# The remainder of the pooled keys in halves of the array's rows, two products of 64 rows in place of each two of 128

## The chip, the core and the metric

The kernel runs on one core of a Trainium2 chip. A core has a matrix engine (TensorE, PE in the profile; its weight loads are listed apart as PEld), three engines for elementwise work (VectorE or DVE, ScalarE or ACT, GpSimd or POOL) and a queue engine (SyncE, SP) that here issues all the transfers. The time of a kernel is the time on the device in microseconds (us); a lower one is better. All times here are of this one core.

## The reference

Attention over pooled keys, followed by a two-layer network with a rational function between the layers. All in float32.

```python
# q, k, v: [8 batches, 8 heads, 576, 64]
k_p = k.reshape(B, H, 72, 8, D).mean(axis=3)      # 72 pooled keys
v_p = v.reshape(B, H, 72, 8, D).mean(axis=3)
scores = scale * np.matmul(q, k_p.transpose(0, 1, 3, 2))
scores = scores - np.max(scores, axis=-1, keepdims=True)
attn = np.exp(scores)
attn = attn / (np.sum(attn, axis=-1, keepdims=True) + 1e-09)
x = np.matmul(attn, v_p)        # -> [4608 tokens, 512]
h = x @ w_in                    # 512 x 2048
P = a[0] + a[1] * h + a[2] * h**2 + a[3] * h**3
Q = 1.0 + np.abs(b[0]) * np.abs(h) + np.abs(b[1]) * h**2
out = (P / (Q + 1e-6)) @ w_out  # 2048 x 512
```

## The kernel before

**Blocks.** The 4608 tokens are 18 blocks of 256 (`TOK`). A batch has 576 tokens, so 12 blocks lie within one batch and 6 straddle two (`segs` then gives two pieces of 64, 128 or 192 tokens). For each block `attend(i)` makes the attention output `x`, transposed, as a high and a low part (`xs`, two tiles in fp32r, the format in which TensorE takes a product in one pass); then eight steps u follow, each with `mm1` (24 products into a bank `ph`), `rational` (ACT, POOL and DVE) and `mm2` (24 products with the weights `wout` into the two banks `po`).

**Attention of a block.** Heads go in four pairs j. A tile of 128 queries gets its scores in banks `ps` (products with the pooled keys `kpT`, full float32, two passes each), then maximum, exponential, sum and quotient on DVE, ACT and POOL in the tile `e`. A pair of heads has 2 x 72 = 144 pooled keys. 128 of them fill the rows of the array; 16 (`REM`) are left over. The probabilities are turned so that the keys lie on the rows: by products with the identity (`pm`, `pr`) in the first four blocks, by DVE transposes and small transfers (`am<-e`) in the later ones. `am0` holds the high parts, `am1` the low parts and, behind them, two columns of tiles for the remainder.

**The remainder before.** For each two pairs (c = 0, 1) the 16 + 16 left-over keys stand four times on the 128 rows: row 32 g + 16 m + r is copy g of key r of pair 2c + m. The copies carry high and low parts, of the probabilities in `am1` and of the values in `vr`, so that one product gives the sum of the part products. `vr` has one 128 x 64 tile for each pair j, in which the rows of the other pair are zero (masks `mrem_lo[m]`, `mrem[m]`, made by `make_masks`, lines 398 to 418; `split_v`, lines 592 to 598, uses them on ACT and DVE).

**`values(i, hi, lo)`** (lines 707 to 729) is where the block's output is summed. There are two banks `pv`, one for each c. For each bank, each jj and each piece of tokens four products follow each other: high values x high probabilities, low x high, the remainder, high x low.

```python
terms = ((o, vh[:, j, :], hi[:, j, r0:r1]), (o, vl[:, j, :], hi[:, j, r0:r1]),
         (pv[:D, jj, r0:r1], vr[n % 2][:, j, :], lo[:, NJ + c, r0:r1]),
         (o, vh[:, j, :], lo[:, j, r0:r1]))
```

The remainder has 128 rows and 64 columns (the left-over keys belong to the first head of the pair), all others 128 x 128. A block has 16 products, or 32 if it straddles, of which 4 or 8 are remainders: 12 x 4 + 6 x 8 = 96 in all. The bank of one c goes to `x` by an ACT copy and a DVE subtraction while the other c is on TensorE. In the built program the instructions name the row groups and column groups of the array that they use. The remainder names all four of both, as the 128 x 128 products do; a straddling tile's `ps` products name two of the four column groups (64 queries each), and `pl`, the last 64 rows of the pooled keys in `prep_k`, names two of the four row groups.

**What sets the order.** `Plan` collects every operation with an estimated cost and a due time, and `solve` sets them in order on each engine by a simulation with these costs. Before that `shift` moves the due times of a random 3% of the first 1850 operations, once for each seed in `SHIFTS` (line 111). Where the plan sees TensorE idle up to the first products of `values`, and here and there later, `issue` puts in filler products (line 276: `idle<-identr`, `po<-zero`). All recorded operations have line 284.

Of the kernel before, what the change touches and what calls it, by code (L numbers as in the profile page):

```python
# [100 lines left out]
class Plan:  # L101
# [9 lines left out]
    SHIFTS = (600170, 650652, 293686, 721265, 222299, 972752, 932340, 238443, 467684, 409349, 642869, 707107)  # L111
# [191 lines left out]
def tile_pooled_attention_then_rational_moe(  # L303
# [80 lines left out]
    masks = new("cpool", "masks", [P, 6], F32, "masks")  # L384
# [6 lines left out]
    mrem_lo, mrem = ([masks[:, i + m:i + m + 1] for m in range(2)] for i in (2, 4))  # L391
# [6 lines left out]
    def make_masks():  # L398
        def band(m, lo, hi):

            small("memset", m, 1.0 / G)
            if lo > 0:
                small("affine_select", out=m, in_=m, pattern=[[0, 1]], compare_op=ALU.is_ge,
                      fill=0.0, base=-lo, channel_multiplier=1)
            if hi < P:
                small("affine_select", out=m, in_=m, pattern=[[0, 1]], compare_op=ALU.is_ge,
                      fill=0.0, base=hi - 1, channel_multiplier=-1)

        band(mlo, 0, SP - REM)
        band(mhi, SP - REM, P)  # L410

        for m in range(2):
            for g in range(4):
                band(bands[:, g:g + 1], g * 32 + m * REM, g * 32 + (m + 1) * REM)
            small("tensor_tensor", out=mrem_lo[m], in0=bands[:, 1:2], in1=bands[:, 3:4],
                  op=ALU.add)
            small("tensor_tensor", out=mrem[m], in0=bands[:, 0:1], in1=bands[:, 2:3], op=ALU.add)
            small("tensor_tensor", out=mrem[m], in0=mrem[m], in1=mrem_lo[m], op=ALU.add)
# [65 lines left out]
    vr = [new("cpool", f"vr{i}", [P, NJ, D], F32R, f"vr{i}") for i in range(2)]  # L484
# [53 lines left out]
    def prep_v_early(n):  # L538
# [11 lines left out]
        for m in range(2):  # L550
            dma(64, place[m * REM:(m + 1) * REM, CW:2 * CW].rearrange("p (c x) -> p c x", c=2),
                rows[m::2, 0:REM, :].rearrange("c r x -> r c x"))
# [5 lines left out]
    def prep_v(n):  # L558
# [4 lines left out]
        for c in (2, 0, 1):  # L563
            place = new("stage", "st", [P, 1024], F32, f"st_v{n}_{c}")
            st = place.rearrange("p (j x) -> p j x", j=2)
            if c < 2:
                dma(512, st, rows[2 * c:2 * c + 2, REM:, :].rearrange("j r x -> r j x"))
            else:
                for g in range(4):
                    for m in range(2):  # L570
                        p0 = g * 32 + m * REM
                        dma(64, place[p0:p0 + REM].rearrange("p (j x) -> p j x", j=2),
                            rows[m::2, 0:REM, :].rearrange("c r x -> r c x"))
# [10 lines left out]
    def split_v(n, vs, vrs, port):  # L584
# [44 lines left out]
    def attention(t, hi, lo, qs, es):  # L629

# [50 lines left out]
        rem = [pairs[:, 2 * c:2 * c + 2, 0:REM].unsqueeze(1).to_broadcast([P, 4, 2, REM])  # L681
               for c in range(2)]
        four = [pairs[:, NJ + c, REM:].rearrange("p (g m r) -> p g m r", g=4, m=2)
# [6 lines left out]
        else:  # L690
# [6 lines left out]
            for c in range(2):  # L697
# [4 lines left out]
            act(2 * P).copy(lo[:, NJ:, col], pr)  # L702
            dve(2 * P).tensor_tensor(
                out=lo[P // 2:, NJ:, col], in0=pr[P // 2:],
                in1=lo[P // 2:, NJ:, col].bitcast(F32), op=ALU.subtract)

    def values(i, hi, lo):

        xs = [new("work2", f"x{s}", [P, NJ, TOK], F32R, f"x{s}_{i}") for s in range(2)]
        for c in range(2):  # L710
            pv = bank(f"pv{i}_{c}", [P, 2, TOK])
            calls = []
            for jj in range(2):
                j = 2 * c + jj
                for r0, r1, n in segs(i * TOK, TOK):
                    vh, vl = vm[n % 2]
                    o = pv[:, jj, r0:r1]
                    terms = ((o, vh[:, j, :], hi[:, j, r0:r1]), (o, vl[:, j, :], hi[:, j, r0:r1]),
                             (pv[:D, jj, r0:r1], vr[n % 2][:, j, :], lo[:, NJ + c, r0:r1]),
                             (o, vh[:, j, :], lo[:, j, r0:r1]))  # L720
                    calls += [mm(dst, vals, probs, s == 0, s == 3)
                              for s, (dst, vals, probs) in enumerate(terms)]
            pe(118 * len(calls), calls, claims=xs)
# [9 lines left out]
    def attend(i):  # L733
# [12 lines left out]
        if i >= 4:  # L746
# [153 lines left out]
    for g in range(4):  # L900
        small("tensor_copy", out=fourfold[:, g * 32:(g + 1) * 32], in_=ident[:2 * REM, :2 * REM])
# [65 lines left out]
```

## Time and profile before

| | us |
|---|---|
| median of 3 runs (lowest, highest) | 943.76 (943.32, 945.35) |
| the profiled execution | 945.64 |
| its span on the core | 943.9 |
| DVE busy in it | 786.0 |
| ACT busy in it | 693.7 |
| POOL busy in it | 528.0 |

The profile is one execution. The median of a group's durations is that of one instruction; products on TensorE are pipelined, so that a product of 256 columns that lasts 0.28 us ends some 0.12 us after the one ahead of it. Costs on TensorE are therefore read from the distance between ends (start plus length of successive rows of the timeline, or the length of a piece in the chain that ended last, divided by its count), not from mean durations. The columns of the views: start, length, engine, line, operation, out<-in, shape (rows * columns of the weights, then the streamed operand), count, and in brackets an idle time and what ended it.

### The profile page before, as it was taken

To read this page: it belongs to the slowest core of one execution; us is meant where nothing else is said; L and a number is where in the kernel's file an instruction comes from. 1 tells how busy PE (TensorE), PEld (TensorE's weight loads), DVE (VectorE), ACT (ScalarE), POOL (GpSimd) and SP (SyncE) were. 2 spreads that over 40 slices of the span, in tenths; PEclk is the share of its full clock that TensorE was granted. 3 is DMA by queue.
4 is the path that set the end of the run, shared out by engine and by line. 5 is a ranking of instruction groups with operands and counts; after the bars stand their busy time and mean duration, and the time that the engine had idled before them with its cause. 6 is when DMAs were issued, how large, how long until landed. Compare 5 with 4: busy or idle time off the path is not lost.

```text
span 943.9 us, 17079 instructions
## 1 busy us (share of the span) xinstructions
PE 932.3 (99%) x6152; PEld 845.0 (90%) x6152; DVE 786.0 (83%) x1336; ACT 693.7 (73%) x1124; POOL 528.0 (56%) x463
## 2 busy tenths in 40 slices
PE   8899999999999999999999999999999999999998
PEld 8888998989988899998999899998999899999996
DVE  7799988788989888887887997888898987887664
ACT  4788889868675877686776777676868595868674
POOL 4776866866446544445634574447545663544443
PEclk9999999999999999999999999999999999999999
DMA  9994201254235322122603160316222421202000
GB/s 275 313 390 160 45 29 46 67 127 87 49 81 105 86 34 47 29 56 53 138 5 75 51 140 8 54 37 139 47 36 50 97 50 28 51 1 57 1 23 23
DMA packets 185365, 75.33 MB, mean 80 GB/s; under 512 B 162624, under 2 KB 162624, under 8 KB 185280
## 3 DMA queue, kind: packets, MB, share of 16 engines
q1 hardware_dynamic: 185280, 74.23, 31.2%
q8 instruction: 49, 0.80, 0.4%
q14 instruction: 36, 0.29, 0.1%
HBM read 50.60 MB, written 12.58 MB: 67 GB/s over the span
## 4 chain that ended last, share of the span: by engine, by line
PE 87%; DMA 3%; SPq 3%; DVE 3%; POOL 1%; ACT 1%; issue 1%; POOLq 0%; ACTq 0%
PE ph L284 39%; PE po L284 39%; PE pv L284 4%; PE ps L284 4%; SPq L284 3%; DMA q<-in_q_dram 1%; DMA early<-in_v_dram 1%; DVE sm L284 1%; DMA st_v<-in_v_dram 1%; DVE t L284 1%; POOL w L284 0%; PE pvs L284 0%; ACT rp L284 0%; PE pq L284 0%; DVE mx L284 0%
## 5 line engine op out<-in xcount | busy, mean ns | idle before, releaser
L284 PEld LDWEIGHTS ph<-x,win 128*128 128x128 f32 x3264 | 472.7, 188 | 55.5 <-ACT w L284 0.8
L284 PE MATMUL ph<-x,win 128*128 128x256 f32 x3264 | 495.7, 282 | 1.4 <-DVE x L284 0.5
L284 PE MATMUL po<-wout,gh 128*128 128x512 f32 x1152 | 353.1, 397 | 0.1
L284 POOL TENSOR_TENSOR w<-w,r 128x512 f32<-128x512 f32 (+1 forms) x145 | 191.1, 1318 | 230.3 <-ACT r L284 228.1
L284 POOL TENSOR_TENSOR gl<-t,gh 128x512 fp32r<-128x512 f32 (+1 forms) x145 | 193.3, 1333 | 93.1 <-ACT gh L284 91.9
L284 PEld LDWEIGHTS po<-wout,gh 128*128 128x128 f32 x1152 | 185.7, 189 | 12.5 <-POOL wout L284 0.8
L284 PE MATMUL po<-wout,gl 128*128 128x512 f32 x576 | 181.8, 396 | 0.3 <-POOL gl L284 0.3
L284 ACT ACTIVATE rp<-w,cbias 128x512 f32<-128x512 f32 (+1 forms) x145 | 99.6, 687 | 59.8 <-POOL w L284 56.6
L284 DVE SCALAR_TENSOR_TENSOR t<-t,abn,rp 128x512 f32<-128x512 f32 (+1 forms) x145 | 107.3, 740 | 38.4 <-ACT rp L284 35.3
L284 DVE TENSOR_TENSOR t<-t,ph 128x512 f32<-128x512 f32 (+1 forms) x145 | 97.8, 675 | 48.7 <-ACT t L284 46.7
L284 ACT ACTIVATE r<-w,abn 128x512 f32<-128x512 f32 (+1 forms) x145 | 117.9, 813 | 20.8 <-POOL gl L284 11.4
L284 ACT ACTIVATE t<-ph,abn 128x512 f32<-128x512 f32 (+1 forms) x145 | 111.0, 767 | 26.3 <-PE ph L284 23.0
L284 ACT ACTIVATE w<-ph 128x512 f32<-128x512 f32 (+1 forms) x145 | 85.7, 591 | 40.8 <-PE ph L284 34.4
L284 DVE SCALAR_TENSOR_TENSOR t<-t,abn,ph 128x512 f32<-128x512 f32 (+1 forms) x145 | 107.0, 738 | 5.2 <-ACT w L284 1.3
L284 ACT CAST gh<-t 128x512 fp32r<-128x512 f32 (+1 forms) x145 | 88.3, 609 | 20.5 <-DVE t L284 16.9
L284 DVE SCALAR_TENSOR_TENSOR t<-rp,t 128x512 f32<-128x512 f32 (+1 forms) x145 | 99.4, 685 | 4.1
L284 DVE SCALAR_TENSOR_TENSOR rp<-w,rp 128x512 f32<-128x512 f32 (+1 forms) x145 | 99.0, 683 | 0.2
L284 PEld LDWEIGHTS po<-wout,gl 128*128 128x128 f32 x576 | 93.0, 189 | 6.4 <-POOL gl L284 0.5
L284 ACT ACTIVATE rp<-rp 128x512 f32<-128x512 f32 (+1 forms) x145 | 84.1, 580 | 3.6 <-DVE t L284 0.5
L284 POOL TENSOR_TENSOR e<-e,sm 128x576 f32<-128x576 f32 x36 | 41.8, 1175 | 51.2 <-DVE sm L284 38.7
L284 POOL TENSOR_TENSOR st_v<-st_v 128x512 f32<-128x512 f32 (+1 forms) x36 | 36.3, 1015 | 17.4 <-DMA st_v<-in_v_dram 10.7
L284 PE MATMUL ps<-kpT,qT 128*128 128x144 f32 (+1 forms) x320 | 45.6, 292 | 0.4 <-DVE kpT L284 0.2
(101 smaller groups left out, 855.9 us busy)
## 6 DMA issues: line engine op xcount, KB each, us to landing
am<-e SPq DMA_DIRECT2D x224, 48.0 KB, 2.1
out_dram<-ob SPq DMA_DIRECT2D x17, 512.0 KB, 3.1
rwin<-in_moe_w_in_dram SPq DMA_DIRECT2D x8, 1024.0 KB, 11.1
rwout<-in_moe_w_out_dram SPq DMA_DIRECT2D x8, 1024.0 KB, 14.1
st_k<-in_k_dram SPq DMA_DIRECT2D x12, 512.0 KB, 4.8
st_v<-in_v_dram SPq DMA_DIRECT2D x12, 512.0 KB, 4.2
q<-in_q_dram SPq DMA_DIRECT2D x144, 32.0 KB, 2.0
st_v<-in_v_dram SPq DMA_DIRECT2D x48, 64.0 KB, 2.2
```

The lines of the kernel that those rows point to most:

```text
L284: getattr(engines[op.eng], name)(*map(value, args), **{k: value(v) for k, v in kw.items()})
```

## The change

The left-over keys are sorted the other way: for jj = 0, 1 the column of tiles holds pairs jj and 2 + jj, and row 64 m + 16 g + r is copy g of key r of pair 2m + jj. So each pair has a half of the rows to itself, `vr` shrinks from four tiles to two, nothing need be zeroed, and a remainder product takes 64 rows. `values` now fills both banks at once, c alternating, so that the two remainder products of one jj, on rows 0 to 63 and 64 to 127 and into different banks, stand next to each other. The number of products stays 384, 96 of them remainders.

```diff
-    SHIFTS = (600170, 650652, 293686, ...)
+    SHIFTS = (945215, 768360, 653776, 414080)
...
-    vr = [new("cpool", f"vr{i}", [P, NJ, D], F32R, f"vr{i}") for i in range(2)]
+    vr = [new("cpool", f"vr{i}", [P, 2, D], F32R, f"vr{i}") for i in range(2)]
...
-        r = vr[n % 2].rearrange("p (c m) x -> p c m x", m=2)
-        for m in range(2):
-            dst = r[:, :, m, :]
-            act(2 * D + 100).activation(dst, vrs, AF.Copy, scale=mrem_lo[m])
-            dve(2 * D, port=port).scalar_tensor_tensor(
-                out=dst, in0=vrs, scalar=mrem[m], in1=dst.bitcast(F32),
-                op0=ALU.mult, op1=ALU.subtract)
+        r = vr[n % 2]
+        act(2 * D + 100).activation(r, vrs, AF.Copy, scale=mrem_lo)
+        dve(2 * D, port=port).scalar_tensor_tensor(
+            out=r, in0=vrs, scalar=1.0 / G, in1=r.bitcast(F32), op0=ALU.mult, op1=ALU.subtract)
...
-        rem = [pairs[:, 2 * c:2 * c + 2, 0:REM].unsqueeze(1).to_broadcast([P, 4, 2, REM])
+        rem = [pairs[:, c:NJ:2, 0:REM].unsqueeze(2).to_broadcast([P, 2, 4, REM])
                for c in range(2)]
-        four = [pairs[:, NJ + c, REM:].rearrange("p (g m r) -> p g m r", g=4, m=2)
+        four = [pairs[:, NJ + c, REM:].rearrange("p (m g r) -> p m g r", g=4, m=2)
                 for c in range(2)]
...
-        for c in range(2):
-            pv = bank(f"pv{i}_{c}", [P, 2, TOK])
+        pvs = [bank(f"pv{i}_{c}", [P, 2, TOK]) for c in range(2)]
+        for jj in range(2):
             calls = []
-            for jj in range(2):
-                j = 2 * c + jj
...
+            sg = segs(i * TOK, TOK)
+            for r0, r1, n in sg:
+                vh, vl = vm[n % 2]
+                for s, (vals, probs) in enumerate(((vh, hi), (vl, hi), (vr[n % 2], lo), (vh, lo))):
+                    for c in range(2):
+                        j = 2 * c + jj
+                        if s == 2:
+                            half = slice(c * (P // 2), (c + 1) * (P // 2))
+                            calls.append(mm(pvs[c][:D, jj, r0:r1], vals[half, jj, :],
+                                            probs[half, NJ + jj, r0:r1], False, False))
+                        else:
+                            calls.append(mm(pvs[c][:, jj, r0:r1], vals[:, j, :],
+                                            probs[:, j, r0:r1], s == 0, s == 3))
+            pe(118 * 7 * len(sg) + 10, calls, claims=xs)
+        for c, pv in enumerate(pvs):
...
-            half = slice(P // 2, P)
-            act(2 * TOK).copy(lo[0:P // 2, NJ:], whole[0:P // 2, NJ:])
-            own = es[half, 0:2, :, 0:P]
-            both = [x[half, NJ:].rearrange("p c (m s) -> p c m s", m=2) for x in (lo, whole)]
-            act(2 * TOK).copy(own.bitcast(F32R), both[1])
+            own = es[:, 0:2, :, 0:P]
+            both = [x[:, NJ:].rearrange("p c (m s) -> p c m s", m=2) for x in (lo, whole)]
+            act(2 * TOK).activation(own.bitcast(F32R), both[1], AF.Copy, scale=one_lo)
             dve(2 * TOK, port=True).tensor_tensor(
                 out=both[0], in0=both[1], in1=own, op=ALU.subtract)
```

High and low copies now lie in both halves of the rows; so the last steps treat all 128 rows and choose by a mask (`one_lo`), where before the upper and the lower 64 rows were treated apart. That takes one ACT operation out of each of the last 14 blocks, and with the smaller `vr` ACT has 22 instructions fewer in all, DVE 8, POOL 10. The transfers are as many and as large as before.

What the change does to the order, at two places. First TensorE in a block within one batch (block 7), the first half of its `values`; `pv_0` and `pv_1` are the banks of the two c, `am` the probabilities, `vm` and `vr` the values. In a row of the order 64x256 is the size of what is written (64 columns of weights, 256 tokens). Before:

```order
L284 MATMUL po_0_1_4436<-wout_1145,gl_3_4591 128x512
L284 MATMUL pv_0_4682<-am_7_4521,vm_863 128x256
L284 MATMUL pv_0_4682<-am_7_4521,vm_906 128x256
L284 MATMUL pv_0_4682<-am_7_4335,vr_808 64x256
L284 MATMUL pv_0_4682<-am_7_4335,vm_863 128x256
L284 MATMUL pv_0_4682<-am_7_4521,vm_863 128x256
L284 MATMUL pv_0_4682<-am_7_4521,vm_906 128x256
L284 MATMUL pv_0_4682<-am_7_4335,vr_808 64x256
L284 MATMUL pv_0_4682<-am_7_4335,vm_863 128x256
L284 MATMUL pv_1_4694<-am_7_4521,vm_863 128x256
```

With the change, at the same place:

```order
L284 MATMUL ph_7_4599<-x_6_4087,win_1864 128x256 x4
L284 MATMUL pv_0_4633<-am_7_4471,vm_843 128x256
L284 MATMUL pv_1_4635<-am_7_4471,vm_843 128x256
L284 MATMUL pv_0_4633<-am_7_4471,vm_922 128x256
L284 MATMUL pv_1_4635<-am_7_4471,vm_922 128x256
L284 MATMUL pv_0_4633<-am_7_4286,vr_977 64x256
L284 MATMUL pv_1_4635<-am_7_4286,vr_977 64x256
L284 MATMUL pv_0_4633<-am_7_4286,vm_843 128x256
L284 MATMUL pv_1_4635<-am_7_4286,vm_843 128x256
```

The two remainder products of a jj stood four apart, each alone between 128-row products; now they are neighbours, and ahead of and behind the two stands a 128 x 128 product. In the built program the first of them names row groups 0 and 1 and the second row groups 2 and 3; both name all column groups. No pair has another pair as its neighbour, so there are 48 such places.

Second, TensorE at the start, where the first block's `values` meets `pq` (the turning of the second block's queries, which waits for the transfer of `q`; `pr` is the last turning of the first block's probabilities, `idle` are fillers). Before:

```order
L284 MATMUL pr_344<-identr,e_240 128x128 x2
L276 MATMUL idle<-identr 128x256 x22
L284 MATMUL idle<-identr 128x128
L284 MATMUL pq_390<-identr,q_256 128x128 x4
L284 MATMUL pv_0_397<-am_0_340,vm_302 128x256
L284 MATMUL pv_0_397<-am_0_340,vm_305 128x256
L284 MATMUL pv_0_397<-am_0_350,vr_313 64x256
```

With the change:

```order
L284 MATMUL pr_336<-identr,e_230 128x128 x2
L284 MATMUL pv_0_353<-am_0_306,vm_291 128x256
L284 MATMUL pv_1_355<-am_0_306,vm_291 128x256
L284 MATMUL pv_0_353<-am_0_306,vm_294 128x256
L284 MATMUL pv_1_355<-am_0_306,vm_294 128x256
L284 MATMUL pv_0_353<-am_0_339,vr_303 64x256
L284 MATMUL pv_1_355<-am_0_339,vr_303 64x256
L284 MATMUL pv_0_353<-am_0_339,vm_291 128x256
L284 MATMUL pv_1_355<-am_0_339,vm_291 128x256
L284 MATMUL pq_367<-identr,q_246 128x128 x4
L284 MATMUL pv_0_353<-am_0_306,vm_291 128x256
```

Half of the first block's `values` now stands ahead of the first `pq`, where fillers were; the other half stands behind it.

Third, a dozen rows further on TensorE, at the second `pq` (the second tile of that block; `ps` are the scores of its first tile, and later of its second). Before:

```order
L284 MATMUL pv_0_397<-am_0_350,vm_302 128x256
L284 MATMUL ps_0_409<-kpT_99,qT_406 128x144 x2
L284 MATMUL ps_1_417<-kpT_99,qT_406 128x144 x2
L284 MATMUL pq_424<-identr,q_256 128x128 x4
L284 MATMUL pv_1_431<-am_0_340,vm_302 128x256
```

With the change:

```order
L284 MATMUL pv_1_355<-am_0_339,vm_291 128x256
L284 MATMUL ps_0_387<-kpT_99,qT_380 128x144 x2
L284 MATMUL ps_1_390<-kpT_99,qT_380 128x144 x2
L284 MATMUL pq_397<-identr,q_246 128x128 x4
L284 MATMUL ps_0_410<-kpT_99,qT_405 128x144 x2
L284 MATMUL ps_1_415<-kpT_99,qT_405 128x144 x2
```

The eight `values` products that stood between the second `pq` and the scores which need it are gone from there.

The rest of TensorE's order keeps its pattern, with other numbers of steps between; the fillers sink from 76 to 46.

More of the change, by code (lines that the diff above doesn't have):

```diff
@@ L383, in tile_pooled_attention_then_rational_moe @@
     zero = real([P, 1], F32R, tag="zero", name="zero")
-    masks = new("cpool", "masks", [P, 6], F32, "masks")
+    masks = new("cpool", "masks", [P, 4], F32, "masks")
     fourfold = new("work1", "vs", [P, P], F32, "fourfold")[:2 * REM]
@@ L389, in tile_pooled_attention_then_rational_moe @@
     mlo, mhi = masks[:, 0:1], masks[:, 1:2]
-    mrem_lo, mrem = ([masks[:, i + m:i + m + 1] for m in range(2)] for i in (2, 4))
+    one_lo, mrem_lo = masks[:, 2:3], masks[:, 3:4]
     QC = 1.0 + 1e-6
@@ L410, in make_masks @@
         band(mhi, SP - REM, P)
-        for m in range(2):
[L413 to L418, printed above, removed]
+        for g in range(4):
+            band(bands[:, g:g + 1], (2 * g + 1) * REM, (2 * g + 2) * REM)
+        for g in (0, 2):
+            small("tensor_tensor", out=bands[:, g:g + 1], in0=bands[:, g:g + 1],
+                  in1=bands[:, g + 1:g + 2], op=ALU.add)
+        small("tensor_tensor", out=mrem_lo, in0=bands[:, 0:1], in1=bands[:, 2:3], op=ALU.add)
+        for m in range(2):
+            band(bands[:, m:m + 1], (4 * m + 2) * REM, (4 * m + 4) * REM)
+        small("tensor_tensor", out=one_lo, in0=bands[:, 0:1], in1=bands[:, 1:2], op=ALU.add)
+        small("tensor_scalar", out=one_lo, in0=one_lo, scalar1=float(G), scalar2=None,
+              op0=ALU.mult)
     WS = 2.0 ** 8
@@ L551, in prep_v_early @@
             dma(64, place[m * REM:(m + 1) * REM, CW:2 * CW].rearrange("p (c x) -> p c x", c=2),
-                rows[m::2, 0:REM, :].rearrange("c r x -> r c x"))
+                rows[2 * m:2 * m + 2, 0:REM, :].rearrange("c r x -> r c x"))
         st = place[:2 * REM, CW:2 * CW].rearrange("p (c t d) -> p t c d", c=2, t=G)
@@ L701, in attention @@
                          for c in range(2)])
-            act(2 * P).copy(lo[:, NJ:, col], pr)
+            act(2 * P).activation(lo[:, NJ:, col], pr, AF.Copy, scale=one_lo)
             dve(2 * P).tensor_tensor(
-                out=lo[P // 2:, NJ:, col], in0=pr[P // 2:],
-                in1=lo[P // 2:, NJ:, col].bitcast(F32), op=ALU.subtract)
+                out=lo[:, NJ:, col], in0=pr, in1=lo[:, NJ:, col].bitcast(F32), op=ALU.subtract)
     def values(i, hi, lo):
         xs = [new("work2", f"x{s}", [P, NJ, TOK], F32R, f"x{s}_{i}") for s in range(2)]
-        for c in range(2):
-            pv = bank(f"pv{i}_{c}", [P, 2, TOK])
+        pvs = [bank(f"pv{i}_{c}", [P, 2, TOK]) for c in range(2)]
+        for jj in range(2):
             calls = []
-            for jj in range(2):
-                j = 2 * c + jj
[L715 to L723, printed above, removed]
+            sg = segs(i * TOK, TOK)
[13 more added lines that the diff above has]
+        for c, pv in enumerate(pvs):
             cs = slice(2 * c, 2 * c + 2)
@@ L899, in tile_pooled_attention_then_rational_moe @@
     plan.now = 0.0
-    for g in range(4):
-        small("tensor_copy", out=fourfold[:, g * 32:(g + 1) * 32], in_=ident[:2 * REM, :2 * REM])
+    small("tensor_copy", out=fourfold.rearrange("p (m g r) -> p m g r", m=2, g=4),
+          in_=ident[:2 * REM, :2 * REM].rearrange("p (m r) -> p m r", m=2).unsqueeze(
+              2).to_broadcast([2 * REM, 2, 4, REM]))
     make_masks()
```

5 lines of the change are left out of this document (2 added, 3 removed).

## The prediction

> **What bounds the kernel now.** I read the page's busy table and its chain first, then the stretches of the span, who waited for whom on TensorE, and last TensorE's timeline around the products that change.
>
> ```profile
> PE 932.3 (99%) x6152; PEld 845.0 (90%) x6152; DVE 786.0 (83%) x1336; ACT 693.7 (73%) x1124; POOL 528.0 (56%) x463
> PE 87%; DMA 3%; SPq 3%; DVE 3%; POOL 1%; ACT 1%; issue 1%; POOLq 0%; ACTq 0%
> 26.00:90.00 64.00, 61.72 (x443) 55.66 (x441) 54.84 (x94) 53.49 (x91) 47.49 (x32) 1.00 0.91 314
> 240.00:580.00 340.00, 339.13 (x2241) 307.70 (x2239) 293.90 (x511) 248.01 (x401) 181.22 (x151) 1.00 0.30 65
> 580.00:900.00 320.00, 320.00 (x2122) 291.60 (x2122) 264.03 (x454) 230.43 (x371) 163.58 (x133) 1.00 0.23 48
> PE pq L284 <- DMA q<-in_q_dram: 1.6, 2, 1.5
> PE pv L284 <- DVE am L284: 0.7, 2, 0.4
> PE ph L284 <- DVE x L284: 0.5, 1, 0.5
> ...
> PE ps L284 <- ACT kpT L284: 0.2, 1, 0.2
> ```
>
> The stretches list first their length, then the busy time of PE, PEld, DVE, ACT and POOL, and the granted clock, which is 1.00 throughout. From 90 us on TensorE is never without work for long: 339.13 of 340 us, 320.00 of 320. The eleven rows of TensorE's waits from that for `am` (0.7 us) down to that for `kpT` (0.2) add up to 3.8 us; besides them it waits 1.5 us for `q` at 25.6 us and 2.1 at the very start. So time that is added to TensorE's queue, or taken out of it, shows almost whole in the span, and the other engines have 16% or more to spare. Only the first 26 us are otherwise: there it waits for transfers.
>
> **What the remainder costs now.** A block within a batch, and the first remainder rows of a straddling block:
>
> ```profile
> 382.15 1.88 PE pv L284 x16
> 331.56 3.19 PE pv L284 x32
> 381.98 0.39 PE L284 MATMUL pv<-am,vm 128*128 128x256 f32 x2
> 382.21 0.28 PE L284 MATMUL pv<-am,vr 128*64 128x256 f32 x1
> 382.33 0.51 PE L284 MATMUL pv<-am,vm 128*128 128x256 f32 x3
> 331.60 0.25 PE L284 MATMUL pv<-am,vr 128*64 128x192 f32 x1
> 331.69 0.44 PE L284 MATMUL pv<-am,vm 128*128 128x192 f32 x3
> 331.96 0.22 PE L284 MATMUL pv<-am,vr 128*64 128x64 f32 x1
> 332.02 0.56 PE L284 MATMUL pv<-am,vm 128*128 128x64 f32 x3
> L284 PEld LDWEIGHTS pv<-am,vm 128*128 128x128 f32 x288 | 42.2, 190 | 1.5 <-DVE am L284 0.3
> L284 PEld LDWEIGHTS pv<-am,vr 128*64 128x64 f32 x96 | 13.1, 136 | 1.1 <-DVE am L284 1.1
> ```
>
> Sixteen products in 1.88 us are 0.118 us each, and the remainder takes its full share: 382.33 - 382.21 = 0.12. In a straddling block a remainder takes 0.09 (192 tokens) or 0.06 (64; I take 0.06 for 128 too). The other products of such a block take (3.19 - 4 x 0.09 - 4 x 0.06) / 24 = 0.108 however few their tokens. Twice the difference of the two weight loads, 190 - 136 = 54 ns for 64 columns, is 0.108 too, so I read them as bound by their loads. All remainders together are 48 x 0.118 + 16 x (0.09 + 0.06 + 0.06) = 9.0 us. Were each pair to take the time of one, at most some 4 us could be won.
>
> **What a pair on half the rows costs.** No product of before has the new form. The nearest rows are `pl` (64 rows, alone among 128 x 128 products), and the `ps` of a straddling tile (two halves of the columns):
>
> ```profile
> 45.67 2.81 PE ph L284 x24
> 48.48 0.20 PE pl L284
> 48.68 0.67 PE ph L284 x4
> 53.45 1.98 PE pvr L284 x16
> 55.43 0.65 PE po L284 x2
> 27.17 0.98 PE ps L284 x8
> 291.14 0.63 PE L284 MATMUL po<-wout,gh 128*128 128x512 f32 x2
> 291.69 0.71 PE L284 MATMUL ps<-kpT,qT 128*64 128x144 f32 x8
> 292.33 1.92 PE L284 MATMUL ph<-x,win 128*128 128x256 f32 x14
> 378.88 0.46 PE po L284 x2
> ```
>
> *Way back.* Behind `pl` four `ph` took 0.67 us; at 2.81 / 24 = 0.117 they should take 0.47: 0.20 more. Behind `pvr` (32 rows) two `po` took 0.65, elsewhere 0.46: 0.19 more. Behind the `ps` halves fourteen `ph` end 292.33 + 1.92 - 291.69 - 0.71 = 1.85 us later, where 14 x 0.117 = 1.64: 0.21 more. So going back to the whole array costs 0.20 us, whatever the part was.
>
> *Way in.* The eight `ps` halves end 291.69 + 0.71 - 291.14 - 0.63 = 0.63 us behind `po`. A full `ps` takes 0.98 / 8 = 0.122. Run as four pairs side by side the eight are 0.49, so the way in cost 0.14, say 0.15. (Run singly they would need 0.98, more than all of 0.63; this also shows that halves do run side by side.) `pl` agrees: 0.20 for one product of 64 columns.
>
> *A pair of 256 tokens* is then 0.15 in, 0.118 for both products, and 0.20 out: 0.468 in place of 2 x 0.118 = 0.236, or **+0.23 us**. In a straddling block the way out is cheaper, since the next product waited 0.108 for its load anyway and streams only 0.03 to 0.09: I take 0.15. The pair is 0.15 + 0.06 + 0.15 (mean stream of 64, 128, 192 tokens) in place of 2 x 0.07: **+0.22**.
>
> Bounds of this: the way in is worth 0 to 0.17 (`pl`'s 0.20 less its stream), the way out 0 to 0.21, the second product 0 to 0.118. What speaks for the lower ends is that the old remainder has 64 columns and no such cost in the rows above. In the built program it names the whole array, though, while `pl`, `pvr` and the `ps` halves name a part of it, and so does the new pair. I go by the rows of those three. The page "TensorEngine Tiling (Array Packing)" of the Trainium skill, section Tiling Modes, says that changing the tiling mode drains TensorE, and gives no figure. The `pl`, `pvr` and `ps` rows agree; the old remainder, though narrower than its neighbours, shows no such gap.
>
> **The sum.** 24 pairs of 256 tokens and 24 in straddling blocks. The first block's two lie where TensorE waits:
>
> ```profile
> 12.02 13.45 DMA q<-in_q_dram
> 25.60 0.63 PE L284 MATMUL pq<-identr,q 128*128 128x128 f32 x4 [1.49 <-DMA q<-in_q_dram]
> 26.23 0.94 PE pv L284 x8
> 26.27 0.59 ACT L284 COPY qT<-pq 128x512 f32<-128x512 f32 x1 [1.96 <-PE pq L284]
> L284 ACT CAST x<-pv 128x512 fp32r<-128x512 f32 x36 | 20.9, 585 | 6.0 <-PE pv L284 5.4
> ```
>
> - 22 x 0.23 + 24 x 0.22 = +10.3 us on TensorE.
> - At the start half of `values`, 0.94 us, moves ahead of a `pq` that comes no sooner: SP issues `q` behind the same three weight transfers, one of `w_in` in place of one of `w_out`. But then the second `pq` has no `values` behind it, and the scores wait for its copy, 0.59 us and the way there. I count -0.3.
> - ACT loses 22 instructions, DVE 8, POOL 10. None ends a wait of TensorE but the one for `am`, 0.7 us in all; I count 0 to -0.5, taken as 0. The DVE subtraction on 128 rows in place of 64 has as many elements a row. Fillers stand where TensorE has nothing to do. Transfers are the same in number and size. All this: nothing.
> - Both `pv` banks now come free together, so the first is held, and its copy to `x` starts, 0.94 us later than before. Behind the run the order of block 7 has six `po` and eight `ph` products on banks already held, 6 x 0.23 + 8 x 0.117 = 2.3 us, ahead of the first use of the new `x`; the two ACT copies need 2 x 0.585 = 1.2 us. So nothing; if ACT is late and the cover goes, it is up to 0.94 us a block.
> - Other seeds: another order can win at most the 3.8 us of TensorE's waits past 26 us; as much could be lost. Taken as 0, with 3 either way.
>
> Together +10.0: 945.64 + 10.0 = 955.6 for an execution like the profiled one, which lay 1.9 above the median. On the median, 943.76 + 10.0, that is **953.8 us**; its own range is 950 to 957.
>
> **The rivals.**
>
> *Side by side at no cost (faster).* The way in and out does not apply to a product of the fp32r kind on half the rows, and the pair takes the time of one. What speaks for it is the old remainder, which changes the width between whole products without a gap; against it, `pl`, whose neighbours are fp32r too. Each full pair wins 0.112 (the second starts a few ns late), each short one 0.03 in the mean, since two loads of 54 ns are needed anyway: 24 x 0.112 + 24 x 0.03 = 3.4, and 0.3 at the start: 940.1. The kernel is faster as long as in and out together cost less than (3.4 + 0.3) / 48 = 0.08 us a pair; the rows have 0.30 to 0.35. The Trainium skill's page "TensorE: Matmul & The Clock Gate", Part 3, has this rule: a pack of products lasts one product and about 4 ns for each further one, with nothing for the change; by it alone the time would be this one. That halves run together the `ps` rows bear out; that nothing is lost going in and out they don't.
>
> *The cost without the gain.* In and out as priced, but the two products one after the other, as the rows show halves of columns together and never halves of rows. 24 x 0.118 + 24 x 0.05 = 4.0 more: 957.8.
>
> *The change does nothing.* No cost, and no overlap: the pair takes 0.236 as before. 943.5, with the seeds' 3 either way.
>
> **How the numbers follow.** The forecast has a chance of 0.65, the cost without the gain 0.13, side by side at no cost 0.13, nothing 0.09. A measurement of this kernel can tell about 0.2% (1.9 us) from no change. "Nothing" with its 3 us either way falls 0.02 faster, 0.05 within that, 0.02 slower, and 0.01 of the forecast falls within. So faster is 0.13 + 0.02 = 0.15, within 0.05 + 0.01 = 0.06, slower 0.65 + 0.13 - 0.01 + 0.02 = 0.79. The range, 943 to 960, holds the forecast with its seeds, the serial case but for its last few us, and the upper half of "nothing"; left out are the free case (0.13), the lower half of "nothing" (0.045) and the top of the serial one (0.02).
>
> **What would show it.** In the changed profile the `pv` piece of a block within a batch should last 1.88 + 2 x 0.23 = 2.34 us, a straddling one 3.19 + 4 x 0.22 = 4.07; the two `vr` products of a pair should start within 0.02 us of each other, the first should end 0.27 us behind the product ahead of it and not 0.118, and the `vm` behind them should end 0.32 us after them. At 1.66 us for the piece the free case holds, at 2.58 the serial one, at 1.88 nothing has changed. TensorE's waits past 26 us should stay near 4 us, and the ones for `x` should not grow. I am wrong in the sum, too, if waits of TensorE for ACT, DVE or banks grow by several us with the new seeds.

## The result, and the profile after

| | before | after |
|---|---|---|
| median, us (lowest, highest) | 944.09 (943.32, 945.35) | 956.15 (953.45, 958.06) |
| the profiled execution, us | 945.64 | 958.06 |
| its span, us | 943.9 | 956.4 |

The ratio is 1.0124, 95% interval 1.0096 to 1.0153: the kernel became slower by some 12 us, or 1.2%. The medians of before are of all runs on the chip beside the run in question and lie between 943.9 and 944.2.

First the page's busy table and chain of after (busy time, share of the span and count of each engine; the chain's shares), three stretches of the span (length, then busy PE, PEld, DVE, ACT, POOL, the granted clock, DMA share, GB/s), and the waits of TensorE (us in all, times, longest):

```profile
PE 944.1 (99%) x6122; PEld 845.3 (88%) x6122; DVE 786.3 (82%) x1328; ACT 683.6 (71%) x1102; POOL 524.7 (55%) x453
PE 95%; DVE 3%; ACT 1%; POOL 0%; issue 0%; POOLq 0%; ACTq 0%
26.00:90.00 64.00, 60.91 (x424) 53.76 (x424) 53.37 (x93) 54.14 (x91) 46.69 (x34) 0.98 0.86 299
240.00:580.00 340.00, 339.22 (x2205) 304.27 (x2204) 289.00 (x499) 237.93 (x383) 178.47 (x148) 0.99 0.29 65
580.00:900.00 320.00, 320.00 (x2095) 287.45 (x2095) 267.46 (x449) 225.64 (x362) 162.84 (x133) 1.00 0.23 48
PE pv L284 <- DVE am L284: 1.7, 2, 1.2
PE pk L284 <- POOL ks L284: 0.9, 1, 0.9
PE ph L284 <- DVE x L284: 0.8, 1, 0.8
PE po L284 <- ACT gh L284: 0.8, 1, 0.8
```

TensorE has 30 products fewer (6122 for 6152; fillers have gone) and is busy 11.8 us longer. Past 240 us it hardly waits: 339.22 of 340 us and 320.00 of 320, as before. But the granted clock, 1.00 in every stretch of before, is 0.98 and 0.99 in two of these. So the loss has two parts to look for, longer products and a slower clock.

The `values` pieces of the chain (start, length), a block within a batch and two straddling ones, and the timeline of the first. In the row with x31 one record is missing; the other straddling blocks took 4.00 to 4.05, but for that at 233.17, whose end falls into a stretch at half clock:

```profile
388.81 2.33 PE pv L284 x16
334.85 4.00 PE pv L284 x31
233.17 4.30 PE pv L284 x32
388.65 0.64 PE L284 MATMUL pv<-am,vm 128*128 128x256 f32 x4
389.22 0.33 PE L284 MATMUL pv<-am,vr 64*64 64x256 f32 x2
389.48 0.96 PE L284 MATMUL pv<-am,vm 128*128 128x256 f32 x6
390.38 0.33 PE L284 MATMUL pv<-am,vr 64*64 64x256 f32 x2
```

The pair ends 389.22 + 0.33 - 388.65 - 0.64 = 0.26 us behind the product ahead of it; in all 24 pairs of 256 tokens the median distance from the product ahead to the first of the pair is 0.259, from the first to the second 0.003, and from the second to the next whole product 0.316. A product of the whole array takes 0.118. So the two halves of the rows do run together, the way in costs 0.14 us and the way out 0.20, and the piece grew from 1.88 to 2.33.

The clock of after, in stretches cut at its changes:

```profile
20.00:25.00 5.00, 3.60 (x25) 2.73 (x24) 4.65 (x9) 4.78 (x12) 1.25 (x5) 1.00 1.12 295
25.00:28.50 3.50, 3.50 (x18) 3.05 (x17) 1.17 (x1) 2.24 (x5) 3.40 (x2) 0.51 1.02 331
236.60:240.00 3.40, 3.40 (x12) 2.71 (x12) 2.08 (x4) 2.37 (x5) 0.16 (x1) 0.51 0.41 154
332.00:339.00 7.00, 7.00 (x53) 6.18 (x52) 6.17 (x10) 5.21 (x9) 4.13 (x4) 1.00 0.00 0
339.00:342.50 3.50, 3.50 (x15) 3.11 (x14) 2.97 (x5) 0.84 (x2) 0.49 (x1) 0.51 0.00 0
237.27 2.02 PE L284 MATMUL po<-wout,gh 128*128 128x512 f32 x4
239.94 1.15 PE L284 MATMUL po<-wout,gh 128*128 128x512 f32 x4
```

Three times TensorE gets half its clock for about 3.4 us, and four `po` products take 2.02 us there and 1.15 right behind it. Each such stretch costs half its length, 1.7 us. One follows the start, where TensorE was busy for 3.60 of 5 us. The other two come at the end of a straddling `values` (233.2 to 237.5 and 334.9 to 338.9 in the chain), where by the busy column TensorE was never without work (7.00 of 7.00 in the second) but four ways in and four out had just passed. By the clock record of the trace the three begin at 25.03, 236.66 and 339.06 us and last 3.41 us each.

The four executions of after show the price: at a mean granted clock of 1.000, 0.998, 0.996 and 0.995 over the whole execution they took 953.45, 955.33, 956.97 and 958.06 us. A stretch of 3.4 us at half clock takes 3.4 x 0.5 / 954 = 0.0018 off the mean, so I take these for zero to three stretches, at 1.1 to 1.9 us each; only the last was profiled.

### The profile page after: what moved, and what is told of

Its sections match the earlier page's. It is cut to its first block, busy times and chain, and to the rows that moved or that the text cites. A ratio compares the mean times of both kernels' runs of the same rounds, so it can differ in the third digit from the quotient of the medians.

```text
span 956.4 us, 16972 instructions
## 1 busy us (share of the span) xinstructions
PE 944.1 (99%) x6122; PEld 845.3 (88%) x6122; DVE 786.3 (82%) x1328; ACT 683.6 (71%) x1102; POOL 524.7 (55%) x453
## 4 chain that ended last, share of the span: by engine, by line
PE 95%; DVE 3%; ACT 1%; POOL 0%; issue 0%; POOLq 0%; ACTq 0%
PE ph L284 42%; PE po L284 41%; PE pv L284 5%; PE ps L284 4%; DVE sm L284 1%; PE pvs L284 1%; PE idle L276 1%; DVE t L284 0%; DVE e L284 0%; PE pvr L284 0%; PE pq L284 0%; PE pk L284 0%; DVE am L284 0%; PE pm L284 0%; DVE mx L284 0%
## 5 line engine op out<-in xcount | busy, mean ns | idle before, releaser
L284 PEld LDWEIGHTS ph<-x,win 128*128 128x128 f32 x3264 | 479.9, 189 | 59.8 <-DVE x L284 1.0
L284 PE MATMUL ph<-x,win 128*128 128x256 f32 x3264 | 502.7, 282 | 1.5 <-DVE x L284 0.8
L284 PE MATMUL po<-wout,gh 128*128 128x512 f32 x1152 | 357.5, 398 | 0.8 <-ACT gh L284 0.8
L284 POOL TENSOR_TENSOR w<-w,r 128x512 f32<-128x512 f32 (+1 forms) x145 | 188.6, 1300 | 238.3 <-ACT r L284 231.5
L284 POOL TENSOR_TENSOR gl<-t,gh 128x512 fp32r<-128x512 f32 (+1 forms) x145 | 195.5, 1348 | 105.3 <-ACT gh L284 101.8
L284 PE MATMUL pv<-am,vm 128*128 128x256 f32 (+3 forms) x288 | 48.7, 295 | 0.2 <-ACT am L284 0.2
```

The costliest lines, as they stand in the source:

```text
L284: getattr(engines[op.eng], name)(*map(value, args), **{k: value(v) for k, v in kw.items()})
```

## The experiments

| run | way in and out, times | median, us | lowest, highest | ratio to before, 95% interval |
|---|---|---|---|---|
| after itself | 48 | 956.15 | 953.45, 958.06 | 1.0124 (1.0096, 1.0153) |
| old_rows_new_seeds | 0 | 958.18 | 956.76, 958.74 | 1.0145 (1.0131, 1.0159) |
| half_rows_old_seeds | 48 | 957.98 | 956.23, 959.65 | 1.0139 (1.0122, 1.0155) |
| whole_rows_same_order | 0 | 944.21 | 942.94, 945.22 | 1.0000 (0.9991, 1.0009) |
| pairs_apart | 96 | 988.09 | 985.64, 991.16 | 1.0465 (1.0445, 1.0486) |
| pairs_together | 18 | 949.73 | 946.62, 950.27 | 1.0052 (1.0039, 1.0065) |
| together_straddling | 30 | 948.99 | 948.53, 950.03 | 1.0049 (1.0037, 1.0062) |
| together_within | 36 | 956.66 | 952.84, 957.51 | 1.0122 (1.0105, 1.0139) |
| start_filled | 48 | 956.05 | 954.17, 956.85 | 1.0126 (1.0110, 1.0141) |
| together_but_start | 20 | 945.22 | 943.81, 946.51 | 1.0013 (1.0004, 1.0021) |
| rows_of_zeros | 0 | 946.00 | 945.17, 947.20 | 1.0024 (1.0014, 1.0034) |
| rows_of_zeros_filled | 0 | 947.73 | 946.13, 948.70 | 1.0041 (1.0028, 1.0053) |

My theory was that the ways in and out are the cost and the seeds are worth nothing; the rivals, that the new order of the work is the cost, or that the second product of a pair is.

**Is it the seeds?** The kernel before with the four new seeds, and the kernel after with the twelve old ones:

```diff
-    SHIFTS = (600170, 650652, 293686, 721265, ...)
+    SHIFTS = (945215, 768360, 653776, 414080)
```

> The kernel before with the four new seeds alone. Theory (the cost is the way in and out of half the rows, 48 times): the seeds only redraw waits of TensorE that sum to 3.8 us, so 941 to 947 us. Rival (the new order costs most of the 12 us): 950 us or more. On the clock: the profiled execution of the changed kernel has stretches of 3.4 us at half the clock, each worth some 1.7 us; if they come from the thinner work of TensorE around the pairs, this kernel has none in its values; if they come from the new order of the start, with few fillers, it has one near 25 us as well.

Missed by more than 10 us: 958.18. Two of TensorE's three largest waits (the third, 2.2 us, is that at the very start) and two stretches of that run:

```profile
PE ph L284 <- DVE t L284: 4.5, 2, 3.3
PE ps L284 <- ACT qT L284: 1.7, 1, 1.7
26.00:90.00 64.00, 58.92 (x429) 53.40 (x429) 54.91 (x92) 52.29 (x88) 44.40 (x32) 1.00 0.87 299
126.00:142.00 16.00, 11.49 (x62) 10.46 (x62) 14.05 (x21) 9.74 (x16) 7.97 (x6) 0.79 0.34 99
```

Between 126 and 142 us alone TensorE is without work for 4.5 us and then at half clock for 6.8 (0.79 for 1.00 over 16 us: 3.4 us lost). From 26 to 90 it is busy 2.8 us less than before. So another order can cost 14 us, which I had put at 3.

> The changed kernel with the twelve old seeds. Theory: 951 to 958 us, as the changed kernel within the seeds' 3 us either way, and clocks below 1.000 in some of its runs. Rival (seeds): 944 to 947 us.

957.98, in the range of the theory. But the seeds move the due times of operations by their number, and the old and new kernels have different operations; so these two runs don't tell what the seeds of *after* cost in *after*. That needs its very order.

**The very order, with whole rows.** In the kernel after, every remainder product takes all 128 rows; it then adds the keys of both pairs, so the output differs from the reference's. All else, order included, stays.

```diff
-                            half = slice(c * (P // 2), (c + 1) * (P // 2))
+                            half = slice(0, P)
```

> The changed kernel in its very order, each remainder product over all 128 rows again (it then adds up the left-over keys of both pairs of a jj, which is not what the reference computes): no way in or out, and no two side by side. Old rows with the new seeds took 958 us, so an order alone can cost 14 us, more than the theory had allowed. Theory now: the new order itself is good, and the 48 pairs cost 10.3 us plus the stretches at half the clock that follow straddling blocks: 943 to 947 us, pv pieces of 1.88 and 3.19 us, no half-clock stretch behind 30 us. Rival (the order costs most of the 12 us): 950 us or more with the same pv pieces.

```profile
112.62 1.88 PE pv L284 x16
329.62 3.19 PE pv L284 x32
```

944.21, before's own time, with before's pieces. So the new order costs nothing in sum, and the half rows cost 956.15 - 944.21 = 11.9 us in it. Their parts in the two profiled executions, whose spans differ by 956.4 - 942.8 = 13.6: eleven blocks at 2.33 - 1.88 = 0.45, six straddling ones at 4.00 - 3.19 = 0.81, and two more stretches at half clock of 1.7 each (both have one at the start): 5.0 + 4.9 + 3.4 = 13.3.

**More ways in and out.** A whole product is put between the two of each pair:

```diff
                             calls.append(mm(pvs[c][:, jj, r0:r1], vals[:, j, :],
                                             probs[:, j, r0:r1], s == 0, s == 3))
+                calls[-3], calls[-2] = calls[-2], calls[-3]
```

> The changed kernel with a whole-array product put between the two remainder products of each pair: 96 ways in and out in place of 48. Theory: 22 x 0.47 + 24 x 0.36 = 19 us more than the changed kernel, 972 to 980 us, a pv piece of 2.33 + 2 x 0.47 = 3.27 us, and if thin work of TensorE lowers the clock, more stretches at half the clock, up to some 985 us. Rival (the cost belongs to the products and not to the way in and out): 954 to 958 us.

```profile
400.52 3.23 PE pv L284 x16
241.70:248.60 6.90, 6.90 (x21) 5.42 (x21) 3.57 (x6) 3.93 (x7) 0.98 (x2) 0.51 0.20 76
347.50:354.50 7.00, 7.00 (x27) 6.26 (x27) 3.08 (x5) 1.17 (x2) 0.58 (x1) 0.51 0.00 0
```

988.09, above the range. The piece of 3.23 (theory 3.27) shows that the price of a way in and out is right. What I had too small was the clock: it falls seven times after 40 us, in the two rows above for 6.83 us each by the clock record, behind straddling blocks, and its mean is 0.984 in the profiled execution, 0.976 to 0.981 in the others. More changes to part of the array mean more time at half clock.

**Fewer ways in and out.** The remainder products of one block are put together behind the others that can go first, so that the array is divided once a block; the flags for a bank's first and last product move with them. This was done for all blocks (pairs_together), for the straddling ones alone (a further condition `len(calls) == 16`) and for those within a batch alone (`len(calls) == 8`):

```diff
-            for name, args, kw in op.calls:
+            calls = op.calls
+            if op.eng == "pe" and any(c[0] == "matmul" and isinstance(c[2]["lhsT"], Lazy)
+                                      and c[2]["lhsT"].tile.name in ("vr0", "vr1")
+                                      for c in calls):
+                key = calls[0][1][0].tile.name
+                early = [c for c in calls if c[2]["lhsT"].tile.name[:2] == "vm"
+                         and c[2]["rhs"].tile.name.startswith("am0")]
+                pair = [c for c in calls if c[2]["lhsT"].tile.name[:2] == "vr"]
+                late = [c for c in calls if c not in early and c not in pair]
+                if key not in kept:
+                    kept[key] = pair, late
+                    calls = [(m, o, dict(k, start=n < 2, stop=False))
+                             for n, (m, o, k) in enumerate(early)]
+                else:
+                    late = kept[key][1] + late
+                    calls = [(m, o, dict(k, start=False, stop=n < 2)) for n, (m, o, k) in
+                             enumerate((early + kept[key][0] + pair + late)[::-1])][::-1]
+            for name, args, kw in calls:
```

> The changed kernel with all remainder pairs of a block next to each other: 18 ways in and out in place of 48, the same products otherwise. Theory: a block within a batch pays 0.15 + 2 x 0.118 + 0.20 = 0.59 in place of the 0.47 of before, a straddling one 0.15 + 4 x 0.108 (bound by the loads) + 0.15 = 0.73 in place of 0.56, together 11 x 0.11 + 6 x 0.17 = 2.3 us over the kernel before, less 0.3 at the start: 945 to 948 us, its pv piece 2.00 us, the clock at 1.000 in most runs. Rival (a product on half the rows is slow by itself, wherever it stands): 954 us or more.

```profile
382.54 2.00 PE pv L301 x16
233.12 3.15 PE pv L301 x32
```

The piece within a batch came as worked out, 2.00. A straddling one was worked out at 3.19 + 0.17 = 3.36 and took 3.13 to 3.28, no more on average than the whole rows of whole_rows_same_order (3.10 to 3.24). Even so 949.73 is above the range. The execution that was profiled took 946.62 with one stretch at half clock; the four others had a mean clock of 0.994 to 0.996 and took 949.35 to 950.27.

> The changed kernel, the remainder pairs next to each other in the six straddling blocks only. Theory: each straddling pv piece goes from 4.00 to 3.15 us, 5.1 us less, and the half-clock stretches (1.7 us each, in the mean about one a run behind 30 us) go with them: 949 to 951.5 us, clock 1.000 behind 30 us. Rival (the half-clock stretches have nothing to do with straddling blocks): 951 us and still some of them.

```profile
682.51 3.15 PE pv L301 x32
```

948.99, at the lower edge of the range, and in the profiled execution no half clock behind any straddling block, only one stretch at 24.6 us; a mean clock of 0.998 to 1.000 in all five. Against after that is 7.2 us for 18 ways in and out fewer, of which the pieces explain 6 x (4.00 - 3.15) = 5.1. The other 2.1 are of the size of one or two stretches at half clock.

> The changed kernel, the remainder pairs next to each other in the twelve blocks within a batch only. Theory: each of their pv pieces goes from 2.33 to 2.00 us, 11 x 0.33 = 3.6 us less; half-clock stretches still follow some straddling blocks: 951.5 to 954 us. Rival (they come from any block's pairs): some 950.5 us, stretches rarer.

956.66, a miss: the pieces shrank to 2.00 and nothing was gained. TensorE's largest waits but for the first load, and three of the four stretches at half clock in the profiled execution:

```profile
PE ph L301 <- DVE x L301: 1.8, 1, 1.8
PE pq L301 <- DVE t L301: 1.7, 1, 1.7
34.80:38.20 3.40, 3.40 (x18) 3.40 (x17) 1.12 (x2) 2.43 (x6) 3.09 (x5) 0.50 1.02 404
62.00:65.60 3.60, 3.60 (x12) 2.54 (x9) 3.56 (x5) 3.02 (x6) 0.44 (x1) 0.53 1.05 404
792.50:796.00 3.50, 3.50 (x14) 3.21 (x14) 1.89 (x3) 1.69 (x3) 0.07 (x1) 0.51 0.00 0
```

Grouping also delays products in the first two blocks: TensorE waits, and the clock falls at 34.8 and 62.1 us. The other two stretches, at 92.8 and 792.6 us, come behind straddling blocks, which this kernel leaves apart, as two did in after. The mean clock is 0.992 to 0.994 in four executions; the fifth, with 0.998, took 952.84, inside the range.

**The start.** Twelve filler products of zeros go ahead of the first remainder, which waits 1.24 us for `am`:

```diff
+                if op.eng == "pe" and name == "matmul" and isinstance(kw["lhsT"], Lazy) \
+                        and kw["lhsT"].tile.name == "vr0" and not filled:
+                    filled = True
+                    for _ in range(12):
+                        self.nc.tensor.matmul(op.calls[0][1][0].ap(), lhsT=self.filler,
+                                              rhs=self.zeros, start=False, stop=False)
```

> The changed kernel with twelve products of zeros (they add nothing) while the first remainder waits for am at 23 us. Theory: the half-clock stretch at 25 us comes from TensorE's thin work there, without fillers; with them it goes, 0.5 to 1.7 us less: 954 to 956 us. Rival (it has another cause): stretch and time as they were.

The scores of the second block's second tile (the second `ps` of the start), in before, after and this run:

```profile
29.37 1.20 PE L284 MATMUL ps<-kpT,qT 128*128 128x144 f32 x8
```

```profile
24.36 0.33 PE L284 MATMUL pv<-am,vr 64*64 64x256 f32 x2 [1.24 <-DVE am L284]
30.39 1.25 PE L284 MATMUL ps<-kpT,qT 128*128 128x144 f32 x8 [0.73 <-ACT qT L284]
```

```profile
25.00:28.50 3.50, 2.93 (x24) 2.43 (x21) 2.23 (x5) 2.59 (x4) 3.50 (x2) 1.00 1.01 349
28.66 1.25 PE L290 MATMUL ps<-kpT,qT 128*128 128x144 f32 x8 [0.73 <-ACT qT L290]
```

With the clock at 1.00 they end at 29.91, with half the clock (after) at 31.64, in before at 30.57. So the new order does gain 0.7 us at the start, and the clock takes 1.7 back. The profiled execution took 954.17 and was at full clock throughout, behind the straddling blocks too. But the median, 956.05, is after's: three of the four executions had a mean clock of 0.996 to 0.998, and whether the fillers help at all is not shown.

**Grouped, the start left alone.** pairs_together without the first two blocks:

```diff
-            if op.eng == "pe" and any(c[0] == "matmul" and isinstance(c[2]["lhsT"], Lazy)
+            if op.eng == "pe" and op.calls[0][1][0].tile.name[:4] not in ("pv0_", "pv1_") and any(c[0] == "matmul" and isinstance(c[2]["lhsT"], Lazy)
```

> The changed kernel with the pairs of products of 64 rows of one block together, as in pairs_together, but the first two blocks left as they are. Theory: grouping in the straddling blocks alone gave 948.99; the ten other blocks within a batch save one way in and one way out each, 0.33 us by the piece of 2.00 for 2.33, so 949.0 - 3.3 = 945.7, between 945 and 947, with pieces of 2.00 and 3.15 and no stretch of half clock after the start. Rival, grouping within a batch yields nothing or costs (as together_within, 956.66 beside 956.15, would have it if its start was not the reason): 949 or above.

```profile
428.91 2.00 PE pv L301 x16
20.00:25.00 5.00, 3.60 (x25) 2.73 (x24) 4.93 (x8) 4.51 (x11) 1.15 (x2) 1.00 1.13 293
28.28 1.25 PE L301 MATMUL ps<-kpT,qT 128*128 128x144 f32 x8 [0.73 <-ACT qT L301]
```

945.22, as expected: grouping within a batch is worth its 3.3 us once the start is left as it was (948.99 - 945.22 = 3.8), and the miss of together_within was in the main its start: grouping the first two blocks too (pairs_together, 949.73) costs 4.5 us. The row from 20 to 25 us is busy for 3.60 of 5, the same as in after, and here no half clock follows. How full TensorE is over some 5 us does not settle alone whether the clock falls.

**Whole rows with zeros.** The keys stay sorted by pair, but `vr` has a tile for each pair again, with zeros in the other pair's rows, filled once by VectorE; `split_v` works on the two halves of the rows one after the other.

```diff
-    vr = [new("cpool", f"vr{i}", [P, 2, D], F32R, f"vr{i}") for i in range(2)]
+    vr = [new("cpool", f"vr{i}", [P, NJ, D], F32R, f"vr{i}") for i in range(2)]
...
-                            calls.append(mm(pvs[c][:D, jj, r0:r1], vals[half, jj, :],
-                                            probs[half, NJ + jj, r0:r1], False, False))
+                            calls.append(mm(pvs[c][:D, jj, r0:r1], vals[:, j, :],
+                                            probs[:, NJ + jj, r0:r1], False, False))
```

> The changed kernel in its own order, with the pooled keys sorted by pair as there, but with the values of each pair in a tile of their own whose other 64 rows are zero, so that every product of the rest has 128 rows and gives the reference's result. The two products of a pair then go one behind the other. Theory (the ways in and out are the cost, the sorting is not): pieces of 1.88 and 3.19 us as in whole_rows_same_order, whose 944.21 it should repeat within the small work on ScalarE and VectorE that is now issued in two halves: 943 to 945.5. Rival, the sorting costs something by itself (two halves on ScalarE and VectorE, late values): above 947.

> rows_of_zeros with the twelve products of zeros of start_filled ahead of the first product of the rest. Theory: the stretch of half clock at 25 us goes, which is worth 1.7 us where it goes in every run, and nothing else changes: 941.5 to 944. Rival, the stretch only comes later or the twelve products delay what is behind them by as much: 943.5 to 946, with no gain on rows_of_zeros that its interval shows.

946.00 and 947.73: the first half a us above the theory's range, the second above both its ranges. VectorE's decoding of the third weight tile, in whole_rows_same_order and in rows_of_zeros, and what TensorE then waits for in the latter:

```profile
24.84 1.22 DVE L284 SCALAR_TENSOR_TENSOR m_win<-rwin,m_win 128x1024 int32<-128x1024 int32 x1
```

```profile
25.27 3.29 DVE L286 SCALAR_TENSOR_TENSOR m_win<-rwin,m_win 128x1024 int32<-128x1024 int32 x1
PE ps L286 <- ACT qT L286: 2.5, 1, 2.5
```

VectorE's work lies 0.4 us later, the same instruction takes 3.29 us where it took 1.22, and the scores wait 2.5 us for `qT` where they waited 0.7 in after. That is of the size of the 1.8 us between 946.00 and 944.21. It has to do with VectorE's work at the start and not with the ways in and out; what held the instruction up wasn't tried, so that it is the reason is not shown. The twelve fillers didn't help here either; their median is 1.7 us worse.

None of these kernels is shown to beat the one before.

## Why the prediction came out as it did

The forecast was 953.8 (own range 950 to 957, with the rivals 943 to 960) and slower; measured 956.15.

- **The mechanism held.** The way in was put at 0.15 and measured 0.14; the way out 0.20 and 0.20; two products side by side 0.118, with their ends 3 ns apart. The pieces were to be 2.34 and 4.07 and are 2.33 and 4.00 to 4.05. The rival at no cost fell (1.66), as did the serial one (2.58). The rows that carried this were `pl`, `pvr` and the `ps` halves of the kernel before; that the old remainder, 64 columns wide, paid nothing was no guide.
- **The pairs.** +10.3 was forecast. Measured: 22 x 0.225 + 24 x 0.20 = +9.8, and whole_rows_same_order takes the order out of the comparison.
- **The clock was missing from the sum, and this is what it was off by.** I looked at the granted clock of before, 1.00, and took it for given. The one execution of after at a clock of 1.000 took 953.45, 0.35 from the forecast. So close a hit is in part luck: with the pairs and the start as measured the sum would be 9.8 - 0.7 = +9.1 in place of +10.0. The others lost one to three stretches of 1.7 us, which the range took in though the sum had no term for them. The change brings these itself: in the profiled executions none behind a straddling block once its products are together, two in after, seven later stretches, some twice as long, with pairs_apart.
- **The start.** I counted -0.3. At full clock it is -0.7 (start_filled) to -1.0 (together_but_start), and +1.1 in the profiled execution of after, because the clock fell there. "Fillers stand where TensorE has nothing to do" was true of its time and not of its clock, as far as that one execution shows it; by the medians it stays open.
- **The seeds** were taken as 0, "3 either way". In this kernel 0 was right (944.21 in the same order), but the bound was wrong: they can lose 14. The waits that one order has show what another can win, not what it can lose.
- **Waits of TensorE past 26 us** were to stay near 4 us; in after they come to some 4.8, with 0.8 for `gh` and 0.7 for `qT` new, 0.5 more for `ks` and 0.3 more for `x`, which was not to grow. The new order brings that; at 944.21 it costs nothing in sum.
- The rest that was taken as nothing (ACT, VectorE, GpSimd, the banks, the transfers) shows nowhere: whole_rows_same_order has all of it and takes before's time.

**When a stretch at half clock comes.** The traces tell part of it. Where a profiled execution has more than one of these stretches, they begin whole multiples of 3.413 us apart: in after at 25.03, 236.66 and 339.06, which is 62 and 30 steps, in pairs_apart 14, 44, 31, 76, 31 and 31 steps. So within an execution the clock changes on a fixed grid of such steps, and the grid lies elsewhere against the work in each execution. (Before, start_filled and together_but_start show one such stretch only, behind their last work or at its very end; I take their grid from it.) The profiled executions of after, half_rows_old_seeds, together_within and start_filled hold 23 straddling blocks with four ways in and out and their `values` in one piece. Behind six of them the clock fell, and there at least 3.21 us of one step lay within the `values`. Of the 17 others, 15 had at most 3.02 us of any step, two had 3.23 and 3.24. So behind like work it is mostly the place of the grid that decides, which no edit here controls; this was read from the traces afterwards, and no run moves the grid.

What stays open is the start. In after the step ahead of 25.03 is busy for 2.01 of 3.41 us and the clock falls; in together_but_start a step is busy for 2.21, in before even for only 1.93, and it does not.

## What to carry to other kernels

Using half of the array is not free at its edges: a lone pair of 64-row products paid 0.34 us of ways in and out to save at most 0.12, so small products should be left on the whole array with zeros, or gathered into one stretch per block (gathered, the kernel took 945.22 at best, beside before's 943.99). Price such a change from any row of the old profile that already uses part of the array, by the distance between ends and not by mean durations. And where a change thins out TensorE's work for a few us, look at the granted clock in short stretches: a mean of 0.995 hid 5 us here.

## What the runs showed of the hardware

- Two products on different halves of the rows and into different banks end 3 ns apart. The Trainium skill's page "TensorE: Matmul & The Clock Gate", Part 3, gives about 4 ns for a further product in a pack: the trace agrees. The Trainium skill's page "TensorEngine Tiling (Array Packing)", section Tiling Modes, says that a change of mode drains TensorE: the runs agree, at 0.14 us in and 0.20 out.
- The clock goes to half for 3.4 us, or twice that (6.83 in pairs_apart), in several cases behind work that the busy columns show as full. The Trainium skill's page "TensorE: Matmul & The Clock Gate", Part 1, has a window of 3413 ns that runs freely, and half clock after an idle one. The length agrees, and so do the distances of 3.413 us and its multiples. That the window must be idle does not: between 332 and 339 us TensorE is listed as busy for 7.00 of 7.00 us, and the drop follows. The same page of the Trainium skill also says that the number of products that run at half clock at the start varies from run to run, as the window runs freely; here the mean clock of the four executions of after varied, from 0.995 to 1.000.
- Seen over a straddling block, four pairs put together cost about what eight whole remainders did (pieces of 3.13 to 3.28 for 3.10 to 3.24), while the same four apart cost 4.00 to 4.05. In a block within a batch two pairs together still cost 0.12 more (2.00 for 1.88).
- A full-float32 product, of which the text ahead says two passes, takes nearly twice as long per column: 0.122 us for 144 columns (`ps`, 0.98 / 8), where an fp32r product takes 0.118 for 256.
